# A decode step with attention and a gated MLP: the MLP in rows, and the last rows of its output weight loaded in smaller pieces behind the query projection

## The chip, the core and the metric

The kernel runs on one core of a Trainium2 chip. The core has a matrix engine (TensorE, PE in the profile), a vector engine (VectorE, DVE), a scalar engine (ScalarE, ACT), GpSimd (POOL) and SyncE (SP), which here does nothing but issue loads; 16 DMA engines move the data. The metric is the device time of one execution in microseconds. Three runs of the kernel before gave 661.75 to 662.25 us, with a median of 661.86.

## The reference

`x` has 4 rows (one token for each of 4 sequences) of 640 numbers. With `xn` its layer norm, the result is `x + A(xn) + B(xn)`. Everything is bf16 at the interface.

```python
def _A_ref(x, k_cache, v_cache, wq, wo):        # 32 heads of 128, 4096 cached positions
    q = (x @ wq).reshape(B, Sq, Hq, Dh).transpose(0, 2, 1, 3)
    scores = einsum('bhqd,bhkd->bhqk', q, k_cache) * Dh ** (-0.5)
    p = softmax(scores, axis=-1)
    o = einsum('bhqk,bhkd->bhqd', p, v_cache)
    return o.transpose(0, 2, 1, 3).reshape(B, Sq, Hq * Dh) @ wo

def _B_ref(x, w_in, w_sp, b_sp, w_out):         # Fh = 864
    z = gelu(einsum('bsd,df->bsf', x, w_in))    # tanh form, 1728 columns
    z1, z2 = z[..., :Fh], layernorm(z[..., Fh:])
    g = einsum('ts,bsf->btf', w_sp, z2) + b_sp  # one number each, as S = 1
    return einsum('bsf,fd->bsd', z1 * g, w_out) # 864 rows of 640
```

K and V are 4 x 32 x 4096 x 128 each, 134 MB apiece, and are read once. wq is 5.2 MB, wo 5.2 MB, w_in 2.2 MB, w_out 1.1 MB.

## The kernel before

The work is cut into 16 units, one for a sequence and a group of 8 heads. A unit's K is 8 MB, 64 KB in each of 128 partitions; so is its V. K goes through a ring of 7 places of 16 KB a partition (`k_ring`), four to a unit; V has one place for a whole unit (`v_all`). For each quarter of K, VectorE multiplies it by the query (`product`, L537) and folds it in half (`fold_half`, L543), TensorE sums eight slices of it into PSUM (`sums`, L555), and VectorE sums each pair of quarters to scores (`row_sums`, L569). Per unit there follow the maximum, the exponentials (`exps`, L596) and their spreading by head into `p_m` (`by_head`, L607). TensorE then multiplies them with V (`weighted`, L631). After each group of four units the outputs are projected with wo; the last group's wo is loaded in pieces (`load_wo`, L228 and L231) and ends the kernel: its products, a copy (L823) and two stores.

Ahead of this, x is loaded (L101, one load on ACT's queue, into a place of the ring), normalised (L265 to L274), transposed into `xnT` (L289 to L294) and multiplied with wq (`q_ps`, L303, 40 matmuls, then L311). wq and w_in, and five rows a partition of w_out, lie in `v_all` until the first V is loaded; the rest of w_out lies in `p_m`'s buffer, which is free until the first unit's exponentials.

**The loads.** All big loads are issued by SP from one list, `loads`, in its order. `pump` (L207) issues from the head of the list until a load's place in the ring, or in `v_all` (the place `V`), is still marked in `busy`. A place is cleared in the code at the instruction that reads it last, and the load waits for that instruction on the chip. Its head is:

```python
    loads = [k_load(0, 0, 1), k_load(0, 1, 2), (load_w, []), k_load(0, 2, 4), (load_w_few, []), k_load(1)]
```

`W_OUT` (L62) cuts the 864 rows of w_out into parts (lanes, rows a lane, number of loads): 128 lanes of 5 rows and 128 lanes of 1 row, issued by `load_w` behind w_in, and 12 lanes of 8 rows in four loads of three lanes each (every fourth lane), issued by `load_w_few`. Each load raises one of eight semaphores, which are used in rotation, and each load waits until the load that had the same semaphore before it has landed.

**The gated MLP** (`gmlp`, L397) is a generator that is run piece by piece between the steps of unit 0. From the line `with tc.manual_schedule` (L733) on, PE, DVE, ACT and SP run in the order in which the code is written. The first piece runs behind the first quarter's sums: for each of the 14 rows of w_out a lane holds, and for both halves of w_in, five matmuls with a 128-column piece of w_in as the weight and `xnT` as the moving operand, 140 in all (L404). So z lies with its features across the partitions and 4 columns for each row of w_out. Behind the second quarter's fold come the copy to SBUF, gelu's polynomial and tanh (L414 to L423), the products and squares (L427 to L432), a matmul with ones that sums over the partitions (L435), the mean and variance on one partition (L445 to L461), their spreading to all partitions with another matmul (L482), the layer norm, gate and product (L488 to L500), and 28 matmuls into `out_ps` (L503). The two scalars of `w_sp` and `b_sp` are loaded by ACT behind the first query spread (L735, L736) and copied by POOL (L464, L466). Then the place `V` is cleared, and V's first load is issued when w_in and w_out in `v_all` have been read.

Of the kernel before, what the change touches and what calls it, by code (L numbers as in the profile page):

```python
# [9 lines left out]
FP32 = mybir.dt.float32  # L10
BF16 = mybir.dt.bfloat16
# [6 lines left out]
def kernel(  # L18
# [43 lines left out]
    W_OUT = ((P, 5, 1), (P, 1, 1), (12, 8, 4))  # L62
    assert sum(n * r for n, r, _ in W_OUT) == Fh
    NFC = sum(r for _, r, _ in W_OUT)

    def up(n):
        return -(-n // 256) * 256

    PW = sum(up(r * D) for _, r, _ in W_OUT[1:])
# [31 lines left out]
    nc.scalar.dma_start(out=x_bf, in_=A_x.flatten_outer_dims())  # L101
# [7 lines left out]
    w_parts, f0, at_p = [], 0, 0  # L109
    for n, r, t in W_OUT:  # L110
        if f0 == 0:
            room = v_all[0:n, at_v : at_v + r * D]
        else:
            room = p_buf[0:n, at_p : at_p + r * D]
            at_p += up(r * D)
        w_parts.append((room.rearrange("p (k n) -> p k n", k=r), f0, n, r, t))
        f0 += n * r
    nc.sync.dma_start(out=wq_sb, in_=A_wq.rearrange("(p c) n -> p c n", c=DC))

    def load_part(part):  # L120
        w, f0, n, r, t = part
        rows = B_w_out[f0 : f0 + n * r].rearrange("(p k) n -> p k n", k=r)
        for l in range(t):
            nc.sync.dma_start(out=w[l:n:t], in_=rows[l:n:t])

    def load_w():
        nc.sync.dma_start(out=w_in_sb, in_=B_w_in.rearrange("(p c) n -> p c n", c=DC))
        for part in w_parts:
            if part[4] == 1:
                load_part(part)  # L130

    def load_w_few():
        for part in w_parts:
            if part[4] > 1:
                load_part(part)

    w_rows = [
        (w[:, i], f0 + i, n, r) for w, f0, n, r, _ in w_parts for i in range(r)
    ]
# [8 lines left out]
    V = RING  # L148
# [46 lines left out]
    loads = [k_load(0, 0, 1), k_load(0, 1, 2), (load_w, []), k_load(0, 2, 4), (load_w_few, []), k_load(1)]  # L195
# [8 lines left out]
    busy = {V}  # L204
# [78 lines left out]
    wsp_bf = const.tile([1, 1], BF16)  # L283
    bsp_bf = const.tile([1, 1], BF16)
# [14 lines left out]
    for e in range(PAR):  # L299
# [14 lines left out]
        q_rows.append(rows)  # L314

# [65 lines left out]
    gm = {}  # L381
    for name in ("zz", "gw", "gt"):
        gm[name] = work.tile([P, 2, NFC, Bsz], FP32, name=name)
    gm["gz"] = work.tile([P, 3, NFC, Bsz], FP32, name="gz")
    nc.gpsimd.memset(gm["zz"][:], 0.0)
    gm["st"] = work.tile([1, 5 * Bsz], FP32, name="st")
    gm["ac"] = work.tile([1, 2 * Bsz], FP32, name="ac")
    gm["yT"] = work.tile([P, NFC, Bsz], BF16, name="yT")

    by_lanes = []  # L390
    for n, r, _ in W_OUT:
        if by_lanes and by_lanes[-1][0] == n:
            by_lanes[-1] = (n, by_lanes[-1][1] + r)
        else:
            by_lanes.append((n, r))

    def gmlp():  # L397
        zz, gw, gt, gz = (gm[n] for n in ("zz", "gw", "gt", "gz"))
        zT = ps_pv.tile([P, 2, NFC, Bsz], FP32, tag="pv", name="zT")
        for t in range(2):  # L400
            w_t = w_in_sb[:, :, t * Fh : (t + 1) * Fh]
            for k, (_, f, n, r) in enumerate(w_rows):
                for c in range(DC):
                    nc.tensor.matmul(  # L404
                        out=zT[0:n, t, k, :],
                        lhsT=w_t[:, c, f : f + (n - 1) * r + 1 : r],
                        rhs=xnT[:, c, 0:Bsz],
                        start=(c == 0),
                        stop=(c == DC - 1),
                    )  # L410
        yield
        k0 = 0
        for n, ks in by_lanes:
            nc.vector.tensor_copy(  # L414
                out=zz[0:n, :, k0 : k0 + ks, :], in_=zT[0:n, :, k0 : k0 + ks, :]
            )
            k0 += ks
        nc.vector.tensor_tensor(out=gw[:], in0=zz[:], in1=zz[:], op=ALU.mult)
        nc.vector.tensor_scalar(
            out=gw[:], in0=gw[:], scalar1=0.044715, scalar2=1.0, op0=ALU.mult, op1=ALU.add  # L420
        )
        nc.vector.tensor_tensor(out=gw[:], in0=gw[:], in1=zz[:], op=ALU.mult)
        nc.scalar.activation(  # L423
            out=gt[:], in_=gw[:], func=ACT.Tanh, scale=math.sqrt(2.0 / math.pi)
        )
        yield
        nc.vector.tensor_scalar(  # L427
            out=gt[:], in0=gt[:], scalar1=1.0, scalar2=0.5, op0=ALU.add, op1=ALU.mult
        )
        nc.vector.tensor_tensor(out=gz[:, 0:2], in0=zz[:], in1=gt[:], op=ALU.mult)  # L430
        sq = gz[:, 2, :, :]
        nc.vector.tensor_tensor(out=sq, in0=gz[:, 1, :, :], in1=gz[:, 1, :, :], op=ALU.mult)  # L432

        s_ps = ps_m.tile([1, 2, NFC, Bsz], FP32, tag="m", name="ln_ps")
        nc.tensor.matmul(  # L435
            out=s_ps[:], lhsT=ones_sq[:, 0:1], rhs=gz[:, 1:3], start=True, stop=True
        )
        yield
        st, ac = gm["st"], gm["ac"]
        mean_t = st[:, 0:Bsz]  # L440
        ex2_t = st[:, Bsz : 2 * Bsz]
        var_t = st[:, 2 * Bsz : 3 * Bsz]
        rst_t = st[:, 3 * Bsz : 4 * Bsz]
        tmp_t = st[:, 4 * Bsz : 5 * Bsz]
        nc.vector.tensor_reduce(  # L445
            out=st[:, 0 : 2 * Bsz].rearrange("o (s b) -> o s b", s=2),
            in_=s_ps[:].rearrange("o s k b -> o s b k"),
            axis=AX.X,
            op=ALU.add,
        )  # L450
        nc.vector.tensor_scalar(
            out=st[:, 0 : 2 * Bsz],
            in0=st[:, 0 : 2 * Bsz],
            scalar1=1.0 / float(Fh),
            scalar2=None,
            op0=ALU.mult,
        )
        nc.vector.tensor_tensor(out=tmp_t, in0=mean_t, in1=mean_t, op=ALU.mult)
        nc.vector.tensor_tensor(out=var_t, in0=ex2_t, in1=tmp_t, op=ALU.subtract)
        nc.scalar.activation(  # L460
            out=rst_t, in_=var_t, func=ACT.Sqrt, bias=eps_tile[:1], scale=1.0  # L461
        )
        wsp_t = work.tile([1, 1], FP32, name="wsp_t")
        nc.gpsimd.tensor_copy(out=wsp_t[:], in_=wsp_bf[:])  # L464
        bsp_t = work.tile([1, 1], FP32, name="bsp_t")
        nc.gpsimd.tensor_copy(out=bsp_t[:], in_=bsp_bf[:])  # L466
        yield
        nc.vector.reciprocal(out=rst_t, in_=rst_t)
        nc.vector.tensor_scalar(
            out=ac[:, 0:Bsz], in0=rst_t, scalar1=wsp_t[:, 0:1], scalar2=None, op0=ALU.mult  # L470
        )
        nc.vector.tensor_tensor(out=tmp_t, in0=ac[:, 0:Bsz], in1=mean_t, op=ALU.mult)
        nc.vector.tensor_scalar(
            out=ac[:, Bsz : 2 * Bsz],
            in0=tmp_t,
            scalar1=-1.0,
            scalar2=bsp_t[:, 0:1],
            op0=ALU.mult,
            op1=ALU.add,
        )  # L480
        ac_ps = ps_m.tile([P, 2 * Bsz], FP32, tag="m", name="ac_ps")
        nc.tensor.matmul(  # L482
            out=ac_ps[:], lhsT=ones_sq[0:1, :], rhs=ac[:], start=True, stop=True
        )
        ac_sb = work.tile([P, 2 * Bsz], FP32, name="ac_sb")
        nc.scalar.copy(out=ac_sb[:], in_=ac_ps[:])
        yield
        nc.vector.tensor_tensor(  # L488
            out=sq,
            in0=gz[:, 1, :, :],  # L490
            in1=ac_sb[:, None, 0:Bsz].to_broadcast([P, NFC, Bsz]),
            op=ALU.mult,
        )
        nc.vector.tensor_tensor(
            out=sq,
            in0=sq,
            in1=ac_sb[:, None, Bsz : 2 * Bsz].to_broadcast([P, NFC, Bsz]),
            op=ALU.add,
        )
        nc.vector.tensor_tensor(out=gm["yT"][:], in0=gz[:, 0, :, :], in1=sq, op=ALU.mult)  # L500
        for k, (w, _, n, _) in enumerate(w_rows):
            for half in range(2):
                nc.tensor.matmul(  # L503
                    out=out_sum(half),
                    lhsT=gm["yT"][0:n, k, :],
                    rhs=w[:, half * NOH : (half + 1) * NOH],
                    start=False,
                    stop=False,
                )
# [346 lines left out]
```

## Time and profile before

| | us |
|---|---|
| median of three runs | 661.86 |
| profiled execution | 662.09 |
| its span, first to last instruction | 660.2 |
| VectorE busy | 522.6 (79%) |
| TensorE busy with matmuls | 317.0 (48%) |
| ScalarE busy | 29.9 (5%) |
| GpSimd busy | 10.1 (2%) |
| share of the DMA queue of SP in 16 engines' span | 99.1% |
| mean rate of the core's transfers | 428 GB/s |

The page gives busy times by engine, a strip of the span in 40 slices (each digit is tenths of a slice), the DMA queues, the chain of work that ended last, and groups of instructions. In the order of time a line gives its start, its length, the engine (SPq and ACTq are the queues on which loads are issued), the line of the kernel, the operation with output and inputs, the number of instructions put together, and in brackets the idle time of the engine before it and what ended that. In the DMA queues q1 is SP's, q10 is ACT's, and q8 and q14 bring instructions.

### The profile page before, as it was taken

How to read it: one execution, taken by the hardware profiler on the slowest of the kernel's cores; microseconds unless marked ns; L12 is line 12 of the kernel's file. 1: busy time of each engine (PE TensorE's matmuls, PEld its weight loads, DVE VectorE, ACT ScalarE, POOL GpSimd, SP SyncE). 2: the span in 40 equal slices, each digit the busy share in tenths (PEclk: the TensorE clock that was granted, in tenths of full speed). 3: DMA queues.
4: the chain of work that ended last, by engine and by line, in shares of the span. 5: the costliest groups of instructions: out<-in, count | busy, mean ns of one | idle time of the engine just before them, and what ended most of it. 6: DMA issues, size and time to landing. Idle time of an engine off the chain costs nothing.

```text
span 660.2 us, 4777 instructions
## 1 busy us (share of the span) xinstructions
PE 317.0 (48%) x2083; PEld 136.3 (21%) x2083; DVE 522.6 (79%) x276; ACT 29.9 (5%) x73; POOL 10.1 (2%) x20
## 2 busy tenths in 40 slices
PE   0574372526427363452636336263452534737367
PEld 0231121212213121120212112121120211212124
DVE  1767978959597795969959598695969969999950
ACT  0020000000000000000000000000000000000000
POOL 2300000000000000000000000000000000000000
PEclk9757676766767676585767768676685867676785
DMA  9999999999999999999999999999999999999997
GB/s 369 433 461 434 417 441 434 433 437 438 421 445 426 437 430 441 437 422 433 434 441 441 418 437 441 430 441 421 434 441 437 426 421 445 422 427 436 449 409 284
DMA packets 8232, 282.55 MB, mean 428 GB/s; under 512 B 892, under 2 KB 2184, under 8 KB 2568
## 3 DMA queue, kind: packets, MB, share of 16 engines
q1 hardware_dynamic: 8192, 282.25, 99.1%
q8 instruction: 16, 0.26, 0.1%
q10 hardware_dynamic: 20, 0.01, 0.0%
q14 instruction: 4, 0.03, 0.0%
HBM read 282.24 MB, written 0.01 MB: 428 GB/s over the span
## 4 chain that ended last, share of the span: by engine, by line
DMA 62%; DVE 28%; PE 8%; issue 1%; ACT 0%; DVEq 0%
DMA k_ring<-in_A_k_cache_dram 53%; DVE k_ring L537 14%; DVE k_ring L543 7%; PE s_ps L555 6%; DMA v_all<-in_A_v_cache_dram 4%; DMA k_ring<-in_A_wo_dram 3%; DVE s_sb L569 3%; DMA v_all<-in_A_wq_dram 2%; DVE p_m L607 1%; DVE m L578 1%; PE q_ps L303 1%; PE pv L631 1%; PE out_ps L699 1%; DVE p_m L678 1%; DVE mf L580 1%
## 5 line engine op out<-in xcount | busy, mean ns | idle before, releaser
L537 DVE TENSOR_TENSOR k_ring<-k_ring,qbc 128x8192 bf16<-128x8192 bf16 x64 | 282.9, 4420 | 88.5 <-DMA k_ring<-in_A_k_cache_dram 87.9
L555 PE MATMUL s_ps<-k_ring,ident 128*128 128x512 bf16 x512 | 202.2, 566 | 313.8 <-DVE k_ring L543 313.7
L555 PEld LDWEIGHTS <-ident 128*128 128x128 bf16 x512 | 64.0, 130 | 430.0 <-issue 245.4
L543 DVE TENSOR_TENSOR k_ring<-k_ring 128x4096 bf16<-128x4096 bf16 x64 | 145.9, 2280 | 1.1
L631 PE MATMUL pv<-v_all,p_m 128*32 128x512 bf16 x960 | 62.5, 419 | 0.0
L569 DVE TENSOR_REDUCE s_sb<-s_ps 128x128 f32<-128x1024 f32 x32 | 39.0, 1218 | 3.7 <-PE s_ps L555 3.7
L607 DVE TENSOR_TENSOR p_m<-p_c,own 128x2048 bf16<-128x2048 bf16 x16 | 36.6, 2285 | 0.7 <-ACT p_c L596 0.7
L631 PEld LDWEIGHTS <-p_m 128*32 128x32 bf16 x992 | 26.6, 106 | 42.5 <-issue 23.3
L596 ACT ACTIVATE p_c<-s_sb,nm 128x256 bf16<-128x256 f32 x16 | 8.1, 508 | 342.9 <-DVE nm L588 342.9
L662 PEld LDWEIGHTS o_ps<-o_rows,pick 128*128 128x128 f32 x96 | 20.4, 294 | 4.3 <-issue 3.3
L662 PE MATMUL o_ps<-o_rows,pick 128*128 128x128 f32 x96 | 19.1, 367 | 0.0
L643 ACT COPY o_rows<-pv 128x512 f32<-128x512 f32 x16 | 9.4, 586 | 165.7 <-PE pv L631 165.7
L311 DVE TENSOR_SCALAR q_rows<-q_ps 128x512 bf16<-128x512 f32 x2 | 1.4, 692 | 12.8 <-PE q_ps L303 12.8
L817 DVE TENSOR_TENSOR o_n_last<-o_last,rden_all 128x32 bf16<-128x32 f32 x1 | 0.2, 192 | 12.2 <-PE o_last L809 12.2
L303 PE MATMUL q_ps<-v_all,xnT 128*32 128x512 bf16 x40 | 4.5, 630 | 9.3 <-DMA v_all<-in_A_wq_dram 9.3
L527 ACT CAST qbc<-qbc_ps 128x128 bf16<-128x128 f32 x16 | 4.3, 266 | 97.6 <-PE qbc_ps L519 97.6
L578 DVE TENSOR_REDUCE m<-s_sb 128x1 f32<-128x256 f32 x16 | 6.7, 420 | 0.5
L519 PE MATMUL qbc_ps<-q_rows,of_row 128*128 128x128 bf16 x32 | 6.0, 276 | 0.6 <-DVE q_rows L311 0.6
L519 PEld LDWEIGHTS <-of_row 128*128 128x128 bf16 x32 | 4.1, 132 | 8.1 <-issue 7.4
L716 PE MATMUL o_last<-hot,o_rows 128*128 128x8 f32 x32 | 4.9, 279 | 0.7 <-ACT o_rows L643 0.7
L716 PEld LDWEIGHTS o_last<-hot,o_rows 128*128 128x128 f32 x32 | 4.8, 226 | 1.8 <-ACT o_rows L643 1.6
L699 PE MATMUL out_ps<-k_ring,p_m 128*4 128x320 bf16 x48 | 4.0, 309 | 2.1 <-DVE p_m L691 2.1
(87 smaller groups left out, 81.4 us busy)
## 6 DMA issues: line engine op xcount, KB each, us to landing
k_ring<-in_A_k_cache_dram SPq DMA_DIRECT2D x5, 4096.0 KB, 27.2
v_all<-in_A_v_cache_dram SPq DMA_DIRECT2D x2, 4096.0 KB, 28.2
v_all<-in_A_wq_dram SPq DMA_DIRECT2D x1, 5120.0 KB, 15.4
k_ring<-in_A_k_cache_dram SPq DMA_DIRECT2D x2, 2048.0 KB
k_ring<-in_A_v_cache_dram SPq DMA_DIRECT2D x1, 4096.0 KB
k_ring<-in_A_wo_dram SPq DMA_DIRECT2D x3, 1280.0 KB, 20.6
v_all<-in_B_w_in_dram SPq DMA_DIRECT2D x1, 2160.0 KB
k_ring<-in_A_v_cache_dram SPq DMA_DIRECT2D x1, 2048.0 KB
```

The lines of the kernel that those rows point to most:

```text
L303: nc.tensor.matmul(out=q_ps[k * QD : (k + 1) * QD], lhsT=xnT[:, c, :], rhs=wq_v[:, c, k, e], start=(c == 0), stop=(c == DC - 1),)
L519: nc.tensor.matmul(out=qb_ps[:], lhsT=of_row[:, e, b].rearrange("p k f l -> p (k f l)"), rhs=q_rows[e][:, hg, :], start=(e == 0), stop=(e ...
L537: nc.vector.tensor_tensor(out=t, in0=t, in1=qbcs[u][:, None, :].to_broadcast([P, HC, Dh]), op=ALU.mult)
L543: nc.vector.tensor_tensor(out=t[:, :, 0:HD2], in0=t[:, :, 0:HD2], in1=t[:, :, HD2:Dh], op=ALU.add)
L555: nc.tensor.matmul(out=s, lhsT=ident[:], rhs=t[:, :, g * RW : (g + 1) * RW], start=(g == 0), stop=(g == m - 1),)
L569: nc.vector.tensor_reduce(out=scores[u][:].rearrange("p (r c) -> p r c", r=NK)[:, lo : hi + 1 : hi - lo], in_=sums_ps.pop(n // 2)[:], axis ...
L578: nc.vector.tensor_reduce(out=m1[:], in_=scores[u][:], axis=AX.X, op=ALU.max)
L607: nc.vector.tensor_tensor(out=p_m[:, u % 2], in0=p_c.pop(u)[:].rearrange("p (g c) -> p g c", c=CB)[:, :, :, None].to_broadcast([P, NG, CB, HT]
L631: nc.tensor.matmul(out=pvs[u][cg * QD : (cg + 1) * QD, :], lhsT=p_m[:, u % 2, g0 + n].rearrange("p c h -> p (c h)"), rhs=v_at[:, n * CB : ...
L662: nc.tensor.matmul(out=gr[hg][:], lhsT=pick[:, c, Bsz - 1 - b : P + Bsz - 1 - b], rhs=o[:, c, :], start=(b == 0 and c == 0), stop=(b == Bs ...
L699: nc.tensor.matmul(out=out_sum(half), lhsT=o, rhs=wo_sb[:, n, half * NOH : (half + 1) * NOH], start=False, stop=(hg == HG - 1 and n == HT ...
L716: nc.tensor.matmul(out=o_last[0][:, :, :, u % Bsz], lhsT=o[:, c, :], rhs=hot[:, c, :].rearrange("p (k e) -> p k e", e=PAR), start=(c == 0) ...
```

## The change

The MLP is turned round: `xnT` (4 rows, padded to 32) is the weight and w_in the moving operand, so that z has a row of x in a partition and its features in columns. The first 640 features are cut in four runs of 160, which lie in four groups of 32 partitions; the other 224 lie in the first group only. The gelu, the sums for the layer norm (by accumulating activations on ScalarE, then one matmul with a matrix `same` that adds the partitions of one row of x) and the gate are done in that form, 384 columns in each half. Five products write `yb` in blocks of 32 columns, a transpose on VectorE turns each block, and 40 matmuls with `yT` add to `out_ps`.

The rows of w_out are cut into 128 lanes of 5, 16 of 2, 8 of 1, 20 of 5 and 12 of 7. The first three are loaded behind w_in, each in one load. The 20 and the 12 lanes are loaded in four loads each, of 5 and of 3 lanes, into the place in `v_all` where wq lay. A new mark `WQ` in `busy` is cleared behind the query projection. In the list of loads two of the 20-lane loads now stand ahead of the second half of the first K unit; the other two and the four 12-lane loads stand behind it. As two loads of w_out now wait for `WQ`, all that stands behind them in the list does so too. `gw` and `yT` lie in `v_all` as well.

x is loaded in four loads of a row each, and the two scalars of `w_sp` and `b_sp` right behind them, all on ACT's queue. The last group's wo is loaded in seven pieces instead of six.

```diff
-    W_OUT = ((P, 5, 1), (P, 1, 1), (12, 8, 4))
+    W_OUT = (
+        (P, 5, "v", 4, ("first",)),
+        (16, 2, "p", 4, ("first",)),
+        (8, 1, "p", 4, ("first",)),
+        (20, 5, "q", 4, ("low", "low", "then", "then")),
+        (12, 7, "q", 4, ("then", "then", "then", "then")),
+    )
...
-    nc.scalar.dma_start(out=x_bf, in_=A_x.flatten_outer_dims())
+    x_rows = A_x.flatten_outer_dims()
+    for b0, b1 in ((0, 1), (1, 2), (2, 3), (3, 4)):
+        nc.scalar.dma_start(out=x_bf[b0:b1], in_=x_rows[b0:b1])
+    wsp_bf = const.tile([1, 1], BF16)
+    bsp_bf = const.tile([1, 1], BF16)
+    nc.scalar.dma_start(out=wsp_bf[:], in_=B_w_sp[0:1, 0:1])
+    nc.scalar.dma_start(out=bsp_bf[:], in_=B_b_sp[0:1].rearrange("(a b) -> a b", a=1))
...
+    places_w = {
+        "v": (v_all, up(DC * (HD + F))),
+        "p": (p_buf, 0),
+        "q": (v_all, 0),
+    }
...
+    def load_part(part, when):
+        w, f0, n, r, used, at = part
+        rows = B_w_out[f0 : f0 + n * r]
+        if len(at) == 1:
+            if at[0] == when:
+                nc.sync.dma_start(out=w, in_=rows.rearrange("(p k) n -> p k n", k=r))
+            return
+        by_used = rows.rearrange("(q l k) n -> l q k n", l=used, k=r)
+        for l in range(used):
+            if at[l] == when:
+                nc.sync.dma_start(out=w[l::GAP], in_=by_used[l])
...
-    loads = [k_load(0, 0, 1), k_load(0, 1, 2), (load_w, []), k_load(0, 2, 4), (load_w_few, []), k_load(1)]
+    loads = [k_load(0, 0, 1), k_load(0, 1, 2), (load_w, []), (load_w_low, [WQ]), k_load(0, 2, 4), (load_w_few, []), k_load(1)]
...
-    busy = {V}
+    busy = {V, WQ}
...
-            for h0, h1 in ((0, 2), (2, 4), (4, 6), (6, 7)):
+            for h0, h1 in ((0, 1), (1, 2), (2, 4), (4, 6), (6, 7)):
...
+    busy.remove(WQ)
+    pump()
...
     def gmlp():
...
+        for c in range(DC):
+            for g in range(NQ):
+                nc.tensor.matmul(
+                    out=z_w[g * QD : (g + 1) * QD],
+                    lhsT=xnT[:, c, :],
+                    rhs=w_v[:, c, :, g * FN : (g + 1) * FN],
+                    start=(c == 0),
+                    stop=(c == DC - 1),
+                )
...
+        for c in range(DC):
+            nc.tensor.matmul(
+                out=z_r[0:QD],
+                lhsT=xnT[:, c, :],
+                rhs=w_v[:, c, :, NQ * FN : Fh],
+                start=(c == 0),
+                stop=(c == DC - 1),
+            )
+        yield
+        nc.scalar.mul(out=zz[:, :, 0:FN], in_=z_w[:], mul=0.5)
+        nc.scalar.mul(out=zz[0:QD, :, FN:FW], in_=z_r[0:QD], mul=0.5)
+        nc.vector.scalar_tensor_tensor(
+            out=gw, in0=zz[:], scalar=4 * 0.044715, in1=zz[:], op0=ALU.mult, op1=ALU.mult
+        )
+        nc.vector.scalar_tensor_tensor(
+            out=gw, in0=gw, scalar=1.0, in1=zz[:], op0=ALU.add, op1=ALU.mult
+        )
+        nc.scalar.activation(
+            out=gw, in_=gw, func=ACT.Tanh, scale=2 * math.sqrt(2.0 / math.pi)
+        )
+        yield
+        nc.vector.scalar_tensor_tensor(
+            out=zz[:], in0=gw, scalar=1.0, in1=zz[:], op0=ALU.add, op1=ALU.mult
+        )
+        for i, func in enumerate((ACT.Copy, ACT.Square)):
+            nc.scalar.activation(
+                out=gw[:, i], in_=zz[:, 1], func=func, accum_out=ss[:, i : i + 1]
+            )
...
+        nc.vector.tensor_scalar(
+            out=zz[:, 1],
+            in0=zz[:, 1],
+            scalar1=st[:, 6:7],
+            scalar2=st[:, 7:8],
+            op0=ALU.mult,
+            op1=ALU.subtract,
+        )
+        yield
+        k0, f_at = 0, 0
+        for n, r, _, used, _ in W_OUT:
...
+            nc.vector.tensor_tensor(
+                out=to.rearrange("p i (q l) -> p i q l", l=GAP)[:, :, :, 0:used],
+                in0=u,
+                in1=v,
+                op=ALU.mult,
+            )
...
+        nc.vector.transpose(
+            out=yT.rearrange("p k b -> p (k b)"), in_=yb[:].rearrange("p k b -> p (k b)")
+        )
+        k = 0
+        for w, _, _, r, _, _ in w_parts:
+            for i in range(r):
+                for half in range(2):
                     nc.tensor.matmul(
                         out=out_sum(half),
+                        lhsT=yT[0 : w.shape[0], k, 0:Bsz],
+                        rhs=w[:, i, half * NOH : (half + 1) * NOH],
...
-        nc.scalar.dma_start(out=wsp_bf[:], in_=B_w_sp[0:1, 0:1])
-        nc.scalar.dma_start(out=bsp_bf[:], in_=B_b_sp[0:1].rearrange("(a b) -> a b", a=1))
```

More of the change, by code (lines that the diff above doesn't have):

```diff
@@ L128, in load_w, with load_w_low @@
         for part in w_parts:
-            if part[4] == 1:
-                load_part(part)
+            load_part(part, "first")
+    def load_w_low():
+        for part in w_parts:
+            load_part(part, "low")
     def load_w_few():
         for part in w_parts:
[L134 to L139, printed above, removed]
+            load_part(part, "then")
     def run_of(cache, u):
@@ L379 @@
         )
[L381 to L395, printed above, removed]
@@ L397, in gmlp @@
-    def gmlp():
[L398 to L410, printed above, removed]
-        yield
[L412 to L420, printed above, removed]
-        )
-        nc.vector.tensor_tensor(out=gw[:], in0=gw[:], in1=zz[:], op=ALU.mult)
+    FW = FN + FR
@@ L456, in gmlp @@
             op0=ALU.mult,
+            op1=ALU.subtract,
         )
[L458 to L461, printed above, removed]
-        )
-        wsp_t = work.tile([1, 1], FP32, name="wsp_t")
-        nc.gpsimd.tensor_copy(out=wsp_t[:], in_=wsp_bf[:])
-        bsp_t = work.tile([1, 1], FP32, name="bsp_t")
@@ L481, in gmlp @@
[L481 to L509, printed above, removed]
+        yield
```

134 lines of the change are left out of this document (77 added, 57 removed).

## The prediction

> **What bounds the kernel now.** I read the transfer rows of the page first, then the chain that ended last, then the order of time from 15 to 85 us and the last 30 us.
>
> ```profile
> DMA  9999999999999999999999999999999999999997
> GB/s 369 433 461 434 417 441 434 433 437 438 421 445 426 437 430 441 437 422 433 434 441 441 418 437 441 430 441 421 434 441 437 426 421 445 422 427 436 449 409 284
> q1 hardware_dynamic: 8192, 282.25, 99.1%
> q8 instruction: 16, 0.26, 0.1%
> DMA 62%; DVE 28%; PE 8%; issue 1%; ACT 0%; DVEq 0%
> ```
>
> The 16 DMA engines are never short of work; 282.25 MB is the whole time. VectorE, 79% busy, appears in the chain only because the chain follows who freed a slot of the ring. The order of time shows how early each load is asked for:
>
> ```profile
> 16.12 0.33 SPq L164 DMA_DIRECT2D k_ring<-in_A_k_cache_dram  x1
> 20.95 7.95 SPq L124 DMA_DIRECT2D p_m<-in_B_w_out_dram  x4
> 31.96 4.61 PE L404 MATMUL zT<-xnT,v_all 128*128 128x4 bf16 x140
> 32.04 0.34 SPq L164 DMA_DIRECT2D k_ring<-in_A_k_cache_dram  x1
> 37.04 0.27 DVE L418 TENSOR_TENSOR gw<-zz 128x112 f32<-128x112 f32 x1
> 44.48 0.22 DVE L500 TENSOR_TENSOR yT<-gz 128x56 bf16<-128x56 f32 x1
> 44.62 4.42 DVE L537 TENSOR_TENSOR k_ring<-k_ring,qbc 128x8192 bf16<-128x8192 bf16 x1
> 46.29 0.33 SPq L175 DMA_DIRECT2D v_all<-in_A_v_cache_dram  x1
> 63.06 4.43 DVE L537 TENSOR_TENSOR k_ring<-k_ring,qbc 128x8192 bf16<-128x8192 bf16 x1 [4.03 <-DMA k_ring<-in_A_k_cache_dram]
> 75.45 0.33 SPq L164 DMA_DIRECT2D k_ring<-in_A_k_cache_dram  x1
> ```
>
> Only what the engines carry, and whether a load is issued before the stream reaches it, can move the end. So I followed the trace's records of single DMA packets, where an engine's next packet starts 3 to 4 ns before its last one ends, which gives 16 separate chains. All have one rate: a 64 KB packet takes 2418 ns, so eight take 19.3 us. They differ in what else they carry. The four 12-lane loads of w_out are 12 packets of 10,240 B on three chains, four each, 385 ns apiece and back to back. The 16 instruction packets fall in turn on eight other chains and hold one up by 1.43 us each (0.9 us of gap and 0.5 us in the packet behind it). When each chain ends its 8 KB packets of the last V unit, in us:
>
> ```
> three with the 12-lane rows    649.07 649.26 649.56
> eight with instruction packets 648.94 650.11 650.13 650.22 650.33 650.41 650.43 650.74
> the other five                 647.54 648.01 648.30 648.49 649.08
> ```
>
> The latest sets the end: its last packet is at 656.62, then the last products and the store, to 660.2. The mean is 649.41, so perfect levelling of all bytes could give 1.33 us.
>
> **The change, part by part.** The sum is made against the profiled execution, 662.09 us (span 660.2 and 1.89 around it), which is 0.23 above the median of 661.86.
>
> *Rows of w_out on the engines.* Eight 1280 B packets leave every chain (spaced 52 ns, 0.42 us with the closing 4 B packet), and the three-lane packets of 4 x 0.387 leave three chains. The 16-lane load adds a 2560 B packet (about 0.10, between 55 ns for 1280 B and 244 ns for 6400 B); the 8-lane one 0.055 on eight chains; the 20-lane rows, in four loads of five lanes, 4 x 0.246 on five; the 12-lane rows, now 8960 B, 4 x 0.34 on three. By the nearest row a load of n lanes puts one packet on each of n chains. The three thus gain 0.10+0.055+0.98+1.36-0.42-1.55 = +0.53 us, two more +0.72, three -0.27, and the other eight -0.32. The three end at 650.1 at the latest, still ahead of the latest. Which the fourth and fifth chains are, the trace does not show: two of the early five (647.5 to 649.1, +0.72 is hidden) or two of the late eight (+0.4 to +0.7 at the end). I take the first, as the always-first three are outside the eight with instruction packets. [...] So the latest chain wins 0.32 us.
>
> *Instructions.* The rows form needs 25 input and 40 output products where there were 140 and 28: 103 matmuls and as many weight loads fewer, 206 of PE's 4166. At 16 packets that is 260 instructions a packet, so up to one packet less, the 16th, on the chain that was at 648.94: nothing at the end. The other 15 come some 10 to 35 us later, on the same chains: nothing. [...]
>
> *Order of the first loads.* The second half of the first K unit (L164) moves from 16.12 to behind the query products and two loads of 20-lane rows: these wait for the last query product (20.6 us), cost SP 0.82 and 0.67 as at L124, so it issues near 22.5. The queue still holds work to 29.4 to 33.0 on its chains: free. Behind it are six small loads, not four. The load instructions name eight semaphores in rotation, and each load waits for the landing of the one eight before (the 7.95 us above are such waits, the last at 28.2). If x's rows and the two scalars keep their place ahead, the six wait for the scalars or K (25.5), w_in (30.6), the wide w_out (32.5), the small ones (32.7) and a 20-lane load (33), and the next K load, the seventh, issues near 35.5 instead of 32.04. The stream reaches it from 41.1 on, and issue to first packet took 1.0 us for wq: 4.6 us to spare.
>
> *Gated MLP in rows.* PE: 20 products of 320 columns, four at a time, and 5 of 448; by the query rows (40 of 512 in 4.46 us) 1.4 + 1.95 = 3.4 us for 4.61, ready at 35.3. ScalarE's halving of 320 and 448 columns: 0.43 and 0.53 (167 ns at 8, 586 at 512). VectorE f32 pairs cost 217 ns at 56 and 275 at 112, 1.04 ns per column: 0.96 for 768, three times. Tanh 1.25 (296 ns at 112, 508 at 256). Two sums with squares, 0.70 and 0.19 to read each: 1.8. PE 0.53. Then VectorE 0.3, a Sqrt whose table load (1.28) starts after the sums, 1.6, three small operations 0.5, 384 columns 0.4 (0.22 to 0.56), five products of 160, 32, 8, 100 and 84 columns 1.25, a transpose of 640 columns 0.58 (0.46 for 512 at L687). Added up, y is there at 46.7 instead of 44.70, and the next K product starts 2.0 us later. It is hidden by the 4.03 us in which VectorE waited for K ahead of 63.06; beyond that, the K load at 75.45 would slip, and the V stream ahead of it runs to 80 to 82, another 5 us. The 40 output products at 0.15 us (28 took 4.2) end at 52.7, and V's first load, which now waits for all of them, issues then and not at 46.29; it is needed by 59.4. Work bounds from half to double of my 2.0 us leave all of this hidden.
>
> *x row by row.* Four issues on ACT at 0.56 each, and two for the scalars, put x on hand near 5 us instead of 3.0, its transpose at 9 instead of 7; wq lands at 16.1. On one chain x costs up to 4 x 0.055, on an early one if the first three are any guide.
>
> *The last wo load in seven parts.* The last half waits in the rotation for the first 4 KB V load (652.3) and not the 8 KB one (651.1), so its packets are there near 653.5; the late chains reach them at 655.9. Free.
>
> Sum: -0.32, so 661.77 for such an execution and 661.5 for a median.
>
> **Rivals.** *A load is issued too late.* Should the rotation shift by one (a scalar's load counted between), the K load behind the six small ones waits for the first K unit's second half, which lands at 42.9. It issues at 43.3, its first packets come at 44.3, and the latest chain, free at 41.7, stands 2.6 us: 661.86 + 2.6 - 0.3 = 664.1. It decides once that issue is later than 40.1; if instead the moved half waits for w_in, the loss is 1.9 and the time 663.4. For it: seven of eight places of the rotation are used. Against it: no reckoning of the order in the code puts a scalar there.
> *The five-lane loads fall on late engines.* +0.4 to +0.7: 662.4. Against it: the cycle of eight.
> *Small loads stop the stream for all engines.* Eight small loads of 4 x 0.25 + 4 x 0.34 against four of 0.39 would be 0.8 us more on all chains, less 0.3: 662.4. Against it: in the trace thirteen chains went straight on. [...]
> *More than levelling.* The 1.33 us at most and a start with less spread (14.54 to 15.76 when wq ends): 660.4, if every late chain gained; only 0.32 to 0.9 is in reach by the rows.
>
> **How the numbers follow.** Forecast 0.62, the late load 0.16, five lanes on late engines 0.12, stopped stream 0.03, more than levelling 0.07. A measurement of this kernel tells about 0.2% (1.3 us) from no change: 660.5 to 663.2. The forecast and the 662.4 rivals are the same within this, less a little at either side: faster 0.09, same 0.74, slower 0.17. The forecast's own range is 661.1 to 662.0; with the rivals 660.7 to 663.4, which leaves out most of the 664.1 and the far end of the levelling.
>
> **What would show it.** DMA at 9 in every slice to the last but one, VectorE's wait before the first product of unit 1 (63.06) shorter by some 2 us, the second K load near 35, V's near 52; 15 or 16 instruction packets; the latest chain again one of the eight, 0.3 us earlier. A gap in the packets between 31 and 45 us, or a late chain with 6400 B packets, would make it wrong.

## The result, and the profile after

The change makes the kernel slower: 671.06 us (four runs, 670.5 to 671.48) against 661.89 (661.75 to 662.25), a ratio of 1.0137 with a 95% interval of 1.0125 to 1.015. The forecast was 661.5, with a range to 663.4. The profiled execution after took 670.97 us with a span of 669.2; before it was 662.09 and 660.2. The last 8 KB packet of the last V unit landed at 659.68 us and not 650.74, which is 8.94 us later; the profiled time grew by 8.88. So all of it had been lost before that, in the stream of loads, and the end of the kernel is as it was.

The page after, in the strip of transfers, the rate, SP's queue, the instruction packets and the engines' shares of the chain that ended last:

```profile
DMA  9899989999999999999999999999999999999996
GB/s 374 378 438 389 415 337 436 439 432 439 435 432 423 431 428 435 439 436 435 436 431 435 401 470 412 431 439 440 439 439 436 423 423 448 407 439 430 460 404 276
q1 hardware_dynamic: 8152, 282.25, 98.1%
q8 instruction: 15, 0.25, 0.1%
DMA 60%; DVE 29%; PE 8%; issue 1%; SPq 1%; ACT 0%; DVEq 0%
```

The bytes are the same, one instruction packet is gone, and in the second and the sixth slice (17 to 33 us and 84 to 100 us) the strip shows an 8 where it had a 9. The rate falls to 378, 389 and 337 GB/s, in slices that stood at 433, 434 and 441. The order of time after says why; these are the loads and the operations that they wait for:

```profile
13.75 0.88 DVE L289 BATCH_NORM_STATS2 stats<-k_ring 4x6 f32<-4x320 bf16 x2 [13.75 <-DMA k_ring<-in_A_x_dram]
18.19 4.05 PE L325 MATMUL q_ps<-v_all,xnT 128*32 128x512 bf16 x40 [0.33 <-DVE xnT L316]
31.07 1.53 SPq L150 DMA_DIRECT2D v_all<-in_B_w_out_dram  x2
32.64 0.44 SPq L188 DMA_DIRECT2D k_ring<-in_A_k_cache_dram  x1
33.13 4.29 SPq L150 DMA_DIRECT2D v_all<-in_B_w_out_dram  x6
37.53 0.35 SPq L188 DMA_DIRECT2D k_ring<-in_A_k_cache_dram  x1
46.84 1.52 PE L430 MATMUL z_w<-v_all,xnT 128*32 128x320 bf16 x20 [12.65 <-DMA v_all<-in_B_w_out_dram]
60.20 0.84 DVE L531 STREAM_TRANSPOSE v_all<-yb 128x640 bf16<-128x640 bf16 x1
60.97 4.38 DVE L573 TENSOR_TENSOR k_ring<-k_ring,qbc 128x8192 bf16<-128x8192 bf16 x1
64.86 0.33 SPq L199 DMA_DIRECT2D v_all<-in_A_v_cache_dram  x1
87.65 0.33 SPq L188 DMA_DIRECT2D k_ring<-in_A_k_cache_dram  x1
```

Three loads come after the stream has run out of work. The second half of the first K unit (L188) is issued at 32.64 instead of 16.12, the first V (L199) at 64.86 instead of 46.29, the K load that stood at 75.45 at 87.65. Counted from the records of single packets, all 16 engines together are idle for 6.85 us an engine between 2 and 655 us (0.26 before), nearly all of it in three gaps: 31.3 to 33.9, 63.0 to 65.8 and 85.5 to 88.7 us.

Two lines of that listing hold the cause. The first 20-lane load, L150, needs the place where wq lay, which is free when the query products end (18.19 + 4.05 = 22.24), yet it goes out at 31.07. And the MLP's first product, L430, reads `xnT` and w_in, which is there at 31, but waits for a load of *w_out*. The queue's own waits after, with total, count and longest, name what the loads waited for:

```profile
SPq L199 <- DVE v_all L531: 14.8, 1, 14.8
SPq L153 <- DMA v_all<-in_A_wq_dram: 13.8, 1, 13.8
SPq L150 <- DMA v_all<-in_B_w_in_dram: 13.2, 1, 13.2
```

and so does the chain that ended last, taken for the first 70 us (start, length, what):

```profile
0.71 15.41 DMA v_all<-in_A_wq_dram
16.14 14.86 DMA v_all<-in_B_w_in_dram
...
36.77 9.82 DMA v_all<-in_B_w_out_dram
46.59 0.24 issue
46.84 1.52 PE z_w L430 x20
```

These waits are in the program as it was built, whose list of SP's instructions has the following; semaphore 1 is w_in's in this place, 5 is the load's own turn in the rotation.

```
7  L145 p_m<-in_B_w_out_dram 8x640     [waits DMAHW4_49]
8  L150 v_all<-in_B_w_out_dram 5x3200  [waits DMAHW5_49,DMAHW1_49,PE_49]
9  L150 v_all<-in_B_w_out_dram 5x3200  [waits DMAHW6_49]
```

w_in and the 20-lane rows lie in the same buffer, `v_all`, in columns that do not overlap. (In the queue's waits above, L153 is another matter: w_in's load has the semaphore that wq's had, and waits for its turn in the rotation. With x in one load it goes out ahead of 14 us and the first 20-lane load at 31.18 all the same.) The load writes `w[l::GAP]`, every fourth partition, and it is ordered against w_in's load as if it touched w_in's columns; in the same way L430's first weight load waits for seven of the eight load semaphores.

Idle engines are not all. After each of the three gaps the first packet of every engine was slow: at 33.7 us the 32 KB packets took 1.49 to 2.07 us, where 1.21 is usual, and at 65.8 and 86 to 89 us the 64 KB packets took up to 3.34 and 3.37 us for 2.42. Over the span the packets took 3.08 us an engine more than their usual times (1.21 before). Idle and slow packets together, 6.6 + 1.9 = 8.5, are the 8.9 lost within 0.4.

### The profile page after: what moved, and what is told of

Same layout as the page of the kernel before. It is cut to its first block, busy times and chain, and to the rows that moved or that the text cites. A ratio compares the mean times of both kernels' runs of the same rounds, so it can differ in the third digit from the quotient of the medians.

```text
span 669.2 us, 4592 instructions
## 1 busy us (share of the span) xinstructions
PE 310.7 (46%) x1980; PEld 130.7 (20%) x1980; DVE 525.0 (78%) x272; ACT 32.2 (5%) x78; POOL 5.9 (1%) x22
## 4 chain that ended last, share of the span: by engine, by line
DMA 60%; DVE 29%; PE 8%; issue 1%; SPq 1%; ACT 0%; DVEq 0%
DMA k_ring<-in_A_k_cache_dram 47%; DVE k_ring L573 14%; DVE k_ring L579 7%; PE s_ps L591 6%; DMA k_ring<-in_A_v_cache_dram 5%; DVE s_sb L605 3%; DMA v_all<-in_A_wq_dram 2%; DMA v_all<-in_B_w_in_dram 2%; DMA k_ring<-in_A_wo_dram 2%; DMA v_all<-in_B_w_out_dram 1%; DVE p_m L643 1%; DVE m L614 1%; SPq L150 1%; DVE p_m L714 1%; PE out_ps L735 1%
## 5 line engine op out<-in xcount | busy, mean ns | idle before, releaser
L573 DVE TENSOR_TENSOR k_ring<-k_ring,qbc 128x8192 bf16<-128x8192 bf16 x64 | 282.8, 4419 | 81.1 <-DMA k_ring<-in_A_k_cache_dram 80.5
L667 PE MATMUL pv<-v_all,p_m 128*32 128x512 bf16 x960 | 60.9, 411 | 0.0
L698 PEld LDWEIGHTS o_ps<-o_rows,pick 128*128 128x128 f32 x96 | 18.8, 271 | 4.2 <-issue 3.3
L698 PE MATMUL o_ps<-o_rows,pick 128*128 128x128 f32 x96 | 17.7, 345 | 0.0
L430 PE MATMUL z_w<-v_all,xnT 128*32 128x320 bf16 x20 | 1.5, 467 | 12.6 <-DMA v_all<-in_B_w_out_dram 12.6
```

What stands on the lines that cost most here:

```text
L573: nc.vector.tensor_tensor(out=t, in0=t, in1=qbcs[u][:, None, :].to_broadcast([P, HC, Dh]), op=ALU.mult)
L667: nc.tensor.matmul(out=pvs[u][cg * QD : (cg + 1) * QD, :], lhsT=p_m[:, u % 2, g0 + n].rearrange("p c h -> p (c h)"), rhs=v_at[:, n * CB : ...
L698: nc.tensor.matmul(out=gr[hg][:], lhsT=pick[:, c, Bsz - 1 - b : P + Bsz - 1 - b], rhs=o[:, c, :], start=(b == 0 and c == 0), stop=(b == Bs ...
```

## The experiments

Two counts from the packet records stand beside each time: idle us an engine (2 to 655 us of the span), and slow us an engine, the packets' time beyond the usual one of their size (2 to 650 us).

| kernel | us | ratio, 95% interval | idle | slow |
|---|---|---|---|---|
| before | 661.9 | | 0.26 | 1.21 |
| after | 671.06 | 1.0137 [1.0125, 1.015] | 6.85 | 3.08 |
| whole lanes | 664.04 | 1.0034 [1.0021, 1.0046] | 0.16 | 2.62 |
| x in one load | 671.51 | 1.0145 [1.0125, 1.0166] | 6.80 | 3.25 |
| 20 lanes behind K | 669.69 | 1.0118 [1.0098, 1.0138] | 4.89 | 3.76 |
| only 12 lanes strided | 669.14 | 1.0108 [1.0088, 1.0128] | 4.40 | 3.47 |
| before, strided in `v_all` | 666.49 | 1.007 [1.0049, 1.009] | 2.61 | 1.89 |
| MLP in rows alone, strided in `p_m` | 662.93 | 1.0015 [1.0007, 1.0024] | 0.37 | 1.09 |
| the same, neighbouring lanes | 664.90 | 1.0045 [1.003, 1.006] | 0.13 | 2.94 |
| before, 28 lanes | 662.98 | 1.0016 [1.0007, 1.0025] | 0.32 | 1.10 |
| before, x by rows | 662.14 | 1.0005 [0.9995, 1.0015] | 0.29 | 1.03 |
| before, 16 and 20 lanes | 668.58 | 1.0089 [1.0072, 1.0107] | 0.08 | 9.76 |
| before, 24 lanes | 662.24 | 1.0006 [0.9997, 1.0016] | 0.40 | 1.20 |
| before, 16 and 16 lanes | 667.87 | 1.0083 [1.0051, 1.0115] | 0.09 | 5.66 |

**Neighbouring lanes in one load each.** The change with the stride taken away: 20 and 12 neighbouring lanes, each in one load.

```diff
-        (20, 5, "q", 4, ("low", "low", "then", "then")),
-        (12, 7, "q", 4, ("then", "then", "then", "then")),
+        (20, 5, "q", 4, ("low",)),
+        (12, 7, "q", 4, ("then",)),
```

> The changed kernel with the 20 lanes in one load and the 12 lanes in one load, on neighbouring partitions, instead of every fourth lane in four loads each; the rows come to the same places. Theory W (a load into every fourth lane is taken to touch all of v_all, so that it waits for w_in and the MLP's input products wait for it): the first 20-lane load issues near 22.5 us and not 31.07, the input products start near 34 and not 46.84, V's first load issues near 52 and not 64.86, the three gaps in the packets go, and the time is 662.1 (661.6 to 662.8). Theory X (x, on hand at 13.75 instead of 3.0, starves the queue): x is as late as in the changed kernel and the time stays above 669. Theory M (the MLP in rows, 14 us from its first product to y instead of 12.5, starves it): the time stays above 667.

Measured: 664.04 us. Its order of time:

```profile
20.86 0.28 SPq L145 DMA_DIRECT2D v_all<-in_B_w_out_dram  x1
21.18 0.36 SPq L188 DMA_DIRECT2D k_ring<-in_A_k_cache_dram  x1
...
34.08 1.50 PE L430 MATMUL z_w<-v_all,xnT 128*32 128x320 bf16 x20
...
53.08 0.35 SPq L199 DMA_DIRECT2D v_all<-in_A_v_cache_dram  x1
77.37 0.33 SPq L188 DMA_DIRECT2D k_ring<-in_A_k_cache_dram  x1
```

The load goes out behind the query products, K's half at 21.18, the product at 34.08 without a wait, V at 53.08. No gap is left, though the MLP is in rows and x as late as in the change (13.62 us). That gives back 7.0 of the 9.2 us. What remains lies in two slow spells that the expectation did not have: 0.75 us an engine at 29 to 34 us and 0.93 at 41 to 46, while the neighbouring lanes are loaded. (This kernel also has two loads in place of eight, which shifts the rotation. That the stride counts and not the number is shown further below, by the kernel with only the 12 lanes strided.)

**x in one load.**

```diff
-    for b0, b1 in ((0, 1), (1, 2), (2, 3), (3, 4)):
-        nc.scalar.dma_start(out=x_bf[b0:b1], in_=x_rows[b0:b1])
+    nc.scalar.dma_start(out=x_bf, in_=A_x.flatten_outer_dims())
```

> The changed kernel with x in one load of four rows, all else kept. Theory W: x is on hand near 3 us and the query products start at 16.2, but the first 20-lane load still waits for w_in (31.1), the input products still for the last 12-lane load (about 46.5), and the time stays at 670 to 671.5. Theory X: the three gaps shrink by 2 us or more each, 662 to 666. Theory M: unchanged, 670 to 671.

Measured: 671.51 us in two runs. The first 20-lane load goes out at 31.18, the MLP's first product begins at 46.75, V is issued at 64.31. x's late arrival is no cause.

**All four 20-lane loads behind K's half.**

```diff
-        (20, 5, "q", 4, ("low", "low", "then", "then")),
+        (20, 5, "q", 4, ("then", "then", "then", "then")),
```

> The changed kernel with all four 20-lane loads behind the second half of the first K unit, so that this K load is not queued behind loads that wait for w_in. Theory W: the gap at 31 to 34 us goes, worth 2.0 us of idling and 0.6 of slow first packets; the input products still wait for the last 12-lane load, near 44, and the two later gaps stay as the stream and the MLP move forward together: 668.4 (667.5 to 669). Theories X and M: unchanged, 670 to 671.

Measured: 669.69 us, above the expected 667.5 to 669. The order of time:

```profile
17.67 0.35 SPq L188 DMA_DIRECT2D k_ring<-in_A_k_cache_dram  x1
30.86 12.67 SPq L150 DMA_DIRECT2D v_all<-in_B_w_out_dram  x8
43.64 0.37 SPq L188 DMA_DIRECT2D k_ring<-in_A_k_cache_dram  x1
45.36 1.52 PE L430 MATMUL z_w<-v_all,xnT 128*32 128x320 bf16 x20 [10.91 <-DMA v_all<-in_B_w_out_dram]
```

The gap at 31 us is gone, and another came at 41.5 to 44.5 us: with eight small loads between the two K loads, the eighth has the semaphore of K's half and waits until that has landed, so the next K load is issued at 43.64. This is the first rival's mechanism, in a kernel for which it had not been meant. The other two gaps stay, since L430 waits as before.

**Only the 12 lanes strided.** 20 neighbouring lanes in one load, 12 lanes in four.

```diff
-        (20, 5, "q", 4, ("low", "low", "then", "then")),
+        (20, 5, "q", 4, ("low",)),
```

> The changed kernel with the 20 lanes in one load of neighbouring lanes, and the 12 lanes as they were, in four loads of every fourth lane. Theory W: the 20-lane load issues near 21 to 22 us and the gap at 31 us goes; the first 12-lane load still waits for w_in (31), the input products for the last 12-lane load (44 instead of 46.84), and gaps at about 62 and 84 us stay: 668 (667 to 669), with stretched packets near 32 us from the neighbouring lanes. If only the loads issued ahead of K mattered: 664.

Measured: 669.14 us. The 20-lane load goes out at 20.95, and the first strided load, the second load behind it, at 30.92; L430 waits 10.47 us to 44.71, V is issued at 62.27, and the gaps lie at 61.5 to 63.9 and 83 to 86.5. In one kernel the load of neighbours into `v_all` does not wait for w_in, and the strided one does.

**The kernel before with its strided loads in `v_all`.** Neither rows in the MLP nor anything else of the change: only the four loads of three lanes go into wq's place, behind the query products.

```diff
-            room = p_buf[0:n, at_p : at_p + r * D]
+            home = v_all if t > 1 else p_buf
+            room = home[0:n, at_p * (t == 1) : at_p * (t == 1) + r * D]
...
-    loads = [..., k_load(0, 2, 4), (load_w_few, []), k_load(1)]
+    loads = [..., k_load(0, 2, 4), (load_w_few, [WQ]), k_load(1)]
```

> The kernel before, with its four loads of every fourth of 12 lanes put where wq lay in v_all, issued behind the query products and in the same place of the list; MLP, x and all else as before. Theory W: the first of them waits for w_in (31 us), the input products (L404 before) for the last, near 43 to 44 instead of 31.96, V's first load issues near 58 to 60 instead of 46.29, gaps open at about 61 and 81 us, and the time is 666 (664 to 668). Theories X and M: as the kernel before, 661.9.

Measured: 666.49 us (665.93 to 667.06).

```profile
31.07 2.92 SPq L125 DMA_DIRECT2D v_all<-in_B_w_out_dram  x4
34.09 0.36 SPq L165 DMA_DIRECT2D k_ring<-in_A_k_cache_dram  x1
43.87 4.65 PE L407 MATMUL zT<-xnT,v_all 128*128 128x4 bf16 x140 [11.37 <-DMA v_all<-in_B_w_out_dram]
...
58.75 0.33 SPq L176 DMA_DIRECT2D v_all<-in_A_v_cache_dram  x1
82.40 0.33 SPq L165 DMA_DIRECT2D k_ring<-in_A_k_cache_dram  x1
```

The old MLP now waits 11.37 us for the same kind of load, and the K load that stood at 75.45 falls into a gap of 80.5 to 83.9 us. The place of the strided loads alone makes the kernel before 4.6 us slower.

**The MLP in rows alone.** The kernel before with the MLP in rows, x in one load, the scalars late, wo in six pieces; the last 224 rows of w_out on 28 lanes in `p_m`'s buffer, in four loads of seven lanes, every fourth.

```diff
+        (P, 5, "v", 4, ("first",)),
+        (28, 8, "p", 4, ("then", "then", "then", "then")),
```

> The MLP in rows alone: x in one load, the scalars and the last wo as before, and the last 224 rows of w_out on 28 lanes of 8 rows in p_m's buffer (which the MLP's input products do not read), in four loads of every fourth lane, behind the first K unit. Theory W: no gap, the input products start near 32, V's first load issues before 54, and the time is 661.5 (661.2 to 661.9), 0.4 below the kernel before, as 0.42 us of 1280 B rows leaves the chains that end last and the seven-lane loads fall on chains that end early. Theory M: 664 or more.

Measured: 662.93 us, with the first input product at 32.41 and V issued at 47.77. Nothing is late, and yet the time is above the expected 661.2 to 661.9; the 1.0 us against before is explained two kernels further on.

**The same with seven neighbouring lanes a load.**

```diff
-                nc.sync.dma_start(out=w[l::GAP], in_=by_used[l])
+                nc.sync.dma_start(out=w[l * m : (l + 1) * m], in_=by_lane[l * m : (l + 1) * m])
```

> As e4, but each of the four loads takes seven neighbouring lanes. Theory N (loads of few lanes on neighbouring partitions slow the stream, as around 31 and 42 us in e1, where 32 KB packets took 1.9 us instead of 1.2 and 64 KB packets 3.3 instead of 2.4): stretched packets after the small loads near 42 us and 662.5 to 665. If neighbouring lanes do not matter: as e4.

Measured: 664.90 us, 1.97 us more for the same bytes in the same number of packets. Between 41 and 46 us the packets of all engines take 1.85 us an engine too long (0.0 with every fourth lane); the 10,240 B packets take up to 1.25 us and not 0.385, the 64 KB ones up to 4.2. The first experiment's slow spells look the same, and their 0.75 and 0.93 us are 1.7 of the 2.15 us that were left there. That the neighbouring lanes cause them too is inferred from this pair of kernels; in that one the stride was not changed alone.

**The kernel before with 28 lanes.**

```diff
-    W_OUT = ((P, 5, 1), (P, 1, 1), (12, 8, 4))
+    W_OUT = ((P, 5, 1), (28, 8, 4))
```

> The kernel before with its last 224 rows of w_out on 28 lanes of 8 rows in four loads of every fourth lane, instead of 128 lanes of 1 row and 12 of 8. MLP as before. If the end is set by the chains that carry instruction packets, they lose 0.42 us each: 661.5 (661.3 to 661.7). If the seven lanes fall on late chains: 662.4 to 663.

Measured: 662.98 us, as much as the MLP in rows with the same lanes (662.93). So the MLP in rows costs nothing, and the 1.0 us belongs to the 28 lanes. Followed along the 16 chains of packets, the ends of the 8 KB packets of the last V unit are

```
28 lanes: seven with 10,240 B packets  651.46 651.23 650.20 649.22 649.04 648.62 648.51
before:   the latest                   650.74
```

and the two latest of the seven also carry two instruction packets each, at 247 and 611 us and at 205 and 573 us. The end moves by 0.72; the profiled times differ by 0.74 (662.83 and 662.09).

**The kernel before with x by rows and the scalars early.**

```diff
+    for b0, b1 in ((0, 1), (1, 2), (2, 3), (3, 4)):
+        nc.scalar.dma_start(out=x_bf[b0:b1], in_=x_rows[b0:b1])
```

> The kernel before with x in four loads of a row each and the two scalars right behind them. Theory W: x is on hand near 13.7 us, the query products start at 18.1 instead of 16.15, the MLP and V's first load are 2 us later (48.5), all hidden, and the time is 661.9 (661.5 to 662.3). Theory X: 664 or more.

Measured: 662.14 us, no difference that can be told. x by rows, which was on hand at 13.75 us in the change, costs nothing here.

**Levelling the chains of the kernel before.** The first of three: the rows of the 128-lane part spread on 16 neighbouring lanes of one row and 20 lanes of four, in `p_m`'s buffer.

```diff
-    W_OUT = ((P, 5, 1), (P, 1, 1), (12, 8, 4))
+    W_OUT = ((P, 5, 1), (P, 1, 1), (16, 1, 1), (20, 4, 4))
```

> The kernel before with its last 96 rows of w_out on 16 lanes of 1 row in one load and 20 lanes of 4 rows in four loads of every fourth lane, five lanes each, instead of 12 lanes of 8 rows. All chains gain 0.06 us, five of them 4 x 0.2 = 0.8, and the three with the 12-lane rows lose 1.55. If the fourth and fifth chains carry no instruction packets: 661.9 (661.7 to 662.1). If one of them does: 662.5 (662.2 to 662.9), with the latest chain at the end one of the five.

Measured: 668.58 us (666.53 to 671.07), which neither theory had. The engines are hardly ever idle (0.08 us). The windows of this kernel (from and to, length, busy time of PE, PEld, DVE, ACT and POOL with the number of instructions, granted clock, DMA share, GB/s):

```profile
34.00:41.00 7.00, 4.50 (x71) 2.84 (x68) 4.23 (x17) 1.90 (x4) 0.00 (x0) 0.50 1.04 367
46.00:60.00 14.00, 4.87 (x18) 1.57 (x15) 13.97 (x5) 0.00 (x0) 0.00 (x0) 0.50 1.06 374
60.00:75.00 15.00, 3.57 (x8) 0.99 (x7) 5.71 (x3) 0.00 (x0) 0.00 (x0) 0.50 0.99 350
```

and of the kernel before:

```profile
34.00:41.00 7.00, 4.41 (x88) 3.11 (x85) 3.97 (x14) 1.88 (x3) 0.00 (x0) 0.57 1.04 447
46.00:60.00 14.00, 7.04 (x31) 2.40 (x28) 13.00 (x5) 0.00 (x0) 0.00 (x0) 0.62 1.01 437
60.00:75.00 15.00, 5.71 (x15) 1.81 (x14) 11.84 (x8) 0.60 (x2) 0.00 (x0) 0.61 1.00 433
```

The DMA share is full in both, and the rate is 350 to 374 in place of 433 to 447 GB/s. The 64 KB packets on all engines take 2.88 to 2.97 us from 43 to some 80 us, a few of them more, and 2.42 again from 85 us on. A share of busy time does not show this; the rate does. Two more kernels each keep one part of the edit: 24 lanes of four rows without the load on 16 neighbours, and 16 neighbours with 16 lanes of five rows.

```diff
+    W_OUT = ((P, 5, 1), (P, 1, 1), (24, 4, 4))
```

> The kernel before with w_out's last 96 rows on 24 lanes of four rows, W_OUT = ((P, 5, 1), (P, 1, 1), (24, 4, 4)): four loads of every fourth lane, six lanes of 5,120 B in each, and no load on 16 neighbouring lanes. The output is the reference's. It is there for the slow spell of the kernel before with 16 and 20 lanes: no idle engine, but every 32 KB packet at about 1.48 us in place of 1.21 and every 64 KB packet at 2.97 in place of 2.42 from about 33 to 80 us, 9.8 us an engine in all. If the one-row load on 16 neighbouring lanes starts that spell, this kernel has none: all 64 KB packets at 2.42 us, and 662 to 663 us. If the strided loads with another number of lanes than three start it, the spell is here, and 666 to 671 us.

Measured: 662.24 us; from 41 to 74 us every 64 KB packet takes 2.42. Levelling over six lanes gains nothing all the same: the latest chain ends its V at 651.05 for 650.74.

```diff
+    W_OUT = ((P, 5, 1), (P, 1, 1), (16, 1, 1), (16, 5, 4))
```

> The kernel before with w_out's last 96 rows on 16 neighbouring lanes of one row and 16 lanes of five, W_OUT = ((P, 5, 1), (P, 1, 1), (16, 1, 1), (16, 5, 4)): the 16-lane load as in the kernel with 16 and 20 lanes, and four loads of every fourth lane with four lanes of 6,400 B in each, in place of five lanes of 5,120 B. The output is the reference's. If the one-row load on 16 neighbouring lanes starts the slow spell, it is here too: 64 KB packets near 2.97 us from about 43 us on, and 666 to 671 us. If the strided loads start it, four lanes should do so as five did, and this run does not tell the two apart alone, but the kernel with 24 lanes does. If neither is the cause, and only the exact order of the 20-lane kernel's loads is, both kernels take 662 to 663 us.

Measured: 667.87 us, but its ten executions go from 661.75 to 671.11, two of them at 661.75 and 661.77 and the rest at 666.77 and above. In the profiled one (666.77) the 64 KB packets take 2.71 us from 41 to 77 us. So of these three kernels the two with the load on 16 neighbouring lanes have the slow spell, and the one without it has not; with strided loads of six lanes it did not come.

That does not make the 16-lane load the cause. The change has a load on 16 neighbouring lanes too, of two rows, and so have its variants. In three of them (whole lanes, 20 lanes behind K, only 12 lanes strided) K follows it without a gap, and the 64 KB packets between 46 and 60 us take 2.42 us. The second half of K is issued late in both slow kernels, at 20.85 and 20.76 us instead of 16.03 with 24 lanes (the rotation); but whole lanes and only 12 lanes strided issue it at 21.18 and 21.29, without the spell. So neither of the two is enough by itself. What the traces do show is where the spell begins: at 32.9 us, right behind the 16-lane load, whose packets pass among others of 1280 B between 31.2 and 32.9 us. What starts it stays open.

## Why the prediction was wrong

**The step that failed** is in *Order of the first loads*: "these wait for the last query product (20.6 us) ... so it issues near 22.5". The loads waited for w_in's landing too, which made it 32.64. The prediction had priced this place: "if instead the moved half waits for w_in, the loss is 1.9 and the time 663.4". That is the first gap, about 2.0 us idle, with 0.56 us of slow packets behind it. It was named as an aside and given no evidence; the code shows two loads into one buffer, and whether the built program orders them is a question that the kernel before, with its strided loads in another buffer, could not answer.

**The same ordering, taken into the MLP.** *Gated MLP in rows* had the input products ready at 35.3, y at 46.7 and V issued at 52.7. L430 began only at 46.84, behind the last 12-lane load; y came at 60.97, V at 64.86, past the 59.4 at which the stream was to need it (behind the first gap it ran dry at about 63), and this is the second gap. The third follows as the step says ("beyond that, the K load at 75.45 would slip"): VectorE went on at 60.97 and not at 44.62, the load slipped to 87.65, and V, itself late, covered the stream to 85.5 only. The rivals held a late load in one place, at 664.1; that one false order makes three loads late was in none of them. Its parts add up: 6.6 us idle and 1.9 us slow.

**What was sized rightly.** The three VectorE pairs took 0.96 each, as predicted. From the first input product to y it was 60.97 - 46.84 = 14.1 us, and in the kernel with neighbouring lanes, by its transpose at 46.52 + 0.85, 13.3; predicted were 3.4 + 46.7 - 35.3 = 14.8. "Work bounds ... leave all of this hidden" is right for the work: with the order mended, the MLP in rows costs nothing that these runs tell (662.93 against 662.98). 15 instruction packets came, and wo in seven pieces left the end as it was.

**x row by row** was put at nothing in the sum, and in the kernel before it makes no difference that can be told (0.26 us); but its size was wrong: x was on hand at 13.75 us, not near 5. The rows' packets start at 1.64, 5.57, 8.65 and 11.72 us, one for every two of the 40,960 B packets (1.51 us each) of the same chain. A row is two packets, its 1280 B and 4 B that close it, and the trace has each of them in turn with one packet of SP's queue: the second row's 4 B start 1.56 us behind its 1280 B, and the third row 1.52 us behind those, so that a row takes 3.1 us.

**"Small loads stop the stream for all engines"** had a chance of 0.03, against it "in the trace thirteen chains went straight on". That holds for every fourth lane and not for neighbours, which the trace of before does not contain: 1.97 us for the same bytes. Why seven neighbours slow the packets of all engines, by 1.85 us an engine, and seven lanes at a stride of four do not (0.0), no run here shows.

**Levelling.** "The latest chain wins 0.32" rested on few-lane loads falling on early chains. Three lanes do; of seven, two fall on chains with instruction packets (+0.72 at the end), and with six the latest chain ended 0.31 us later, not earlier. The +0.53 and +0.72 of the sum take all four loads of five lanes to fall on the same five chains, three of them those of the 12 lanes; the trace before has the like for loads of three lanes alone, and no run shows an order of the chains in which those three come first. In the trace after, the 6400 B packets of the last two such loads lie end to end in pairs on five chains at 43.9 to 44.9 us, and on three of these the 8960 B packets follow, four on each. Whether the five-lane loads fell on late engines, the second rival, stays open: its 0.4 to 0.7 us cannot be told within the 8.9 that were lost.

## What to carry to other kernels

Before a load is moved into a place of a shared buffer, look up in the built program what that load and the readers of the buffer's other columns wait for: here a load to every fourth partition waited for w_in, whose columns it does not touch (it went out at 31.07 us, its place being free at 22.24), and the first matmul waited 12.65 us for a transfer that it does not read. When one load becomes late, follow the delay to the next loads that are issued behind it and behind what it holds up, as one order cost three gaps (6.6 us idle). A rate beside the busy share tells slow transfers from full ones: 350 to 374 GB/s here for 433 to 447, at a share of 0.99 to 1.06 in both.

## What the runs showed of the hardware

- After each of the change's three gaps the first packets of all engines were slow: 1.49 to 2.07 us for 1.21 at 32 KB, up to 3.37 for 2.42 at 64 KB, 0.55 to 0.8 us an engine and gap.
- With four loads on seven neighbouring lanes each, the packets of all engines took 1.85 us an engine too long between 41 and 46 us; with the same rows on every fourth lane they did not (0.0). In the kernel with whole lanes, loads on 12 and 20 neighbouring lanes come with 0.93 and 0.75 us.
- In the kernel before with 16 and 16 lanes the 64 KB packets took 2.71 us for 2.42 (12% longer) from 41 to 77 us, and with 16 and 20 lanes 2.88 to 2.97 us (19 to 23%) from 43 to some 80, on all engines at once, with hardly any idle time (0.09 and 0.08 us) and a DMA share of 0.98 to 1.06 between 46 and 75 us. By their times, eight of ten executions of the first had this (666.77 us and above) and two had not (661.75 and 661.77). What starts and ends it is open.
